# Holding each batch's loads to its tile, and reordering the first feed-forward tile, in an attention and ReGLU kernel

## The chip, the cores and the metric

The kernel runs on one core of a Trainium2 chip. The metric is the device time of one execution in microseconds; smaller is better. A core has five engines with queues of their own: TensorE (PE, with its weight loads shown as PEld), VectorE (DVE), ScalarE (ACT), GpSimd (POOL) and SyncE (SP). SP, ACT and POOL also issue DMAs. Each queue is worked off in order.

## The reference

Block-causal attention (a query sees the keys of its own block of 64 and of all earlier ones) over 8 batches, 8 heads, 576 positions and a head size of 64, followed by a gated feed-forward layer on all 4608 tokens. Inputs and output are float32.

```python
def _attn_ref(q, k, v):
    scores = scale * np.matmul(q, k.transpose(0, 1, 3, 2))
    mask = block_i >= block_j
    scores = np.where(mask, scores, -1000000000.0)
    scores = scores - np.max(scores, axis=-1, keepdims=True)
    attn = np.exp(scores)
    attn = attn / (np.sum(attn, axis=-1, keepdims=True) + 1e-09)
    return np.matmul(attn, v).astype(np.float32)

def _moe_ref(x, w_gate, w_val, w_out):
    gate = np.maximum(x @ w_gate, 0.0)
    val = x @ w_val
    return (gate * val @ w_out).astype(np.float32)
```

The attention output, transposed to (batch, position, head x size), is x: 4608 x 512. w_gate and w_val are 512 x 1536, w_out is 1536 x 512.

## The kernel before, in words

**Feed-forward tiles.** Everything is computed in bf16 with sums in float32. The 512 leading positions of each batch make one feed-forward tile (tiles 0 to 7); the last 64 positions of all eight batches make tile 8. `ffn_gen` (L566) is a generator that issues one tile after the other, and each `yield` follows one matmul. A tile has 144 such steps: steps 0 to 95 are the products with w_gate and w_val (twelve column groups f, for each four contraction chunks c of gate and four of val; L572), steps 96 to 143 are the products with w_out (four output groups s of twelve steps; L631). After a gate group comes a ReLU on ACT (L582), after a val group a product on DVE that writes hT (L588) and is put in the list `products`. A finished output group is copied to a buffer `ob` on DVE (L665) and stored by a DMA from ACT (L558). In tile 0 the first two output groups are different: their steps f = 0 to 7 go into two banks, are copied into `ob` as side sums (L651), and f = 8 to 11 go into banks of their own and are added to `ob` (L662). In tiles 0 and 1 the groups f = 0 and 1 are interleaved, two of them in score banks.

**Attention rounds.** A round r is one pair of heads of batch r // 4. `visit` (L368) issues its eight score products into two pairs of score banks ("sc") and into a third place (a bank "one" and a bank "ffnp"), and gives back three exponentials on ACT (L391, L397). `corners` (L446) zeroes the masked corners. `head_av` (L504) multiplies one head's weights with v on TensorE (L495) and normalises on DVE (L460, L461) into xnat; `both_av` (L518) does two heads in score banks. xnat is transposed into xT, the feed-forward input, either on TensorE (`to_xT_pe`, L533) or by a transposing DMA from SP (`to_xT_dma`, L544, issued at L547). Round r gives chunk c = r % 4 of the xT of its batch. The last 64 positions of a batch have a `tail_visit`, two `tail_av` and a transposing DMA into xTt (L489).

**PSUM.** Eight banks: two score tiles of two banks ("sc"), one bank "one", three banks "ffnp". The three ffnp banks serve the feed-forward groups, the third place of a visit, the head products with v, the transposes of `pe_mains` and to_xT for two of four rounds.

**Bringing in q, k and v.** Batches 0, 1 and 2 come by float32 loads from SP into ten stage buffers (class `Early`, L107), and are cast to bf16 on POOL, DVE or ACT. For batches 0 and 1 `pe_mains` (L232) transposes q and k of one pair of heads on TensorE and copies them to qTm and kTm (L244) on two engines; `pe_tails` does it for the last 64 positions. Batch 2 is transposed by SP's DMAs into "perm" and unpermuted by DVE and POOL. Batches 3 to 7 are loaded and cast in one step by POOL's DMAs (`load_qkv`, L266: five for q, five for k, five for v, issued at L278), then transposed by `dma_transposes` (L287) from SP. An argument `behind` makes the first DMA of the group wait for a given instruction. The bf16 buffers of q and k are doubled, those of v go by b % 2.

**Weights.** `load_w_half` loads the 512 columns i of w_gate and w_val in two halves of 256 columns, each half for all four contraction chunks, in runs of 1 KB. `load_w` loads w_out in runs of 2 KB. `cast_w` casts a stage buffer on a given engine (L327).

**The order.** The schedule is by hand. Each engine executes in the order in which the program issues. The start (L699 to L782) is written out in full; after it, `run` (L789) takes a list of events, each with a position p (a count of generator steps from a base), advances the generator to base + p and performs the event. A position of 0 to 143 with base 0 is a step of tile 0; tile j has base 144 j. `round_at(p, r, av, to_xT, after)` (L794) makes the events of a round: the visit and its first two exponentials at p, the third at p + after[0], the corners at p + after[1], the products with v at av, the transposition at to_xT. For batches 3 to 7 the loop at L897 places, in the tile before their own, the batch's rounds and, from position 120, its tail events, and also the loads of batch b + 1: q and k at position 9, v at position 46, `dma_transposes(b + 1)` at 66. Only for b = 3 (the loads of batch 4) is the first DMA held behind `products[-1]`, the last product on DVE that the program has issued by then. Positions order an engine against its own queue only; SP and POOL run ahead as far as data and buffers allow.

Of the kernel before, what the change touches and what calls it, by code (L numbers as in the profile page):

```python
# [17 lines left out]
def kernel(  # L18
# [88 lines left out]
    class Early:  # L107
# [124 lines left out]
        def pe_mains(self, hp, evac):  # L232
            for t in range(2):
                tp = psum_ffn.tile([128, 512], BF, name="ffnp")
                src = self.half(t, hp // 2)
                lo = 128 * (hp % 2)
                for j in range(4):
                    nc.tensor.transpose(  # L238
                        tp[:, 128 * j : 128 * j + 128], src[:, j, lo : lo + 128], ident
                    )  # L240
                for eng, c0, c1 in (
                    evac[t] if isinstance(evac[t], list) else [(evac[t], 0, 4)]
                ):
                    eng(  # L244
                        (qTm, kTm)[t][self.b % 2][:, c0:c1, hp, :].rearrange(
                            "p c (n j) -> p c n j", j=4
                        ),
                        tp.rearrange("p (j c n) -> p c n j", j=4, c=4)[:, c0:c1],
                    )
# [68 lines left out]
    def load_w_in(i):  # L318
        cols = slice(512 * i, 512 * i + 512)
        return load_w(wg[i], moe_w_gate[:, cols], 0) + load_w(wv[i], moe_w_val[:, cols], 0)  # L320
# [245 lines left out]
    def ffn_gen():  # L566
        for j in range(B + 1):
# [50 lines left out]
            for f in range(first, 12):  # L618
                gate = psum_ffn.tile([128, 512], FP, name="ffnp")
                val = psum_ffn.tile([128, 512], FP, name="ffnp")  # L620
                for t in range(2):
                    for c in range(4):
                        product((gate, val)[t], t, c, f)
                        if (t, c) == (0, 3):
                            gate_sb = relu(gate)
                        if (t, c) == (1, 3):
                            hidden(gate_sb, val)
                        yield

            def out_mm(op, s, f, n0, n1, lo, hi):  # L630
                nc.tensor.matmul(  # L631
                    op,
                    hT[f][:, 128 * s : 128 * (s + 1)],
                    wo[f // 4][:, f % 4, n0:n1],
                    start=(f == lo),
                    stop=(f == hi - 1),
                )

            def new_ob(n):
                return sb.tile([128, 512], FP, name="ob", bufs=4)[:, 0:n]  # L640

            part_sum = {}
            if j == 0:
                ops = [psum_ffn.tile([128, 512], FP, name="ffnp") for _ in range(2)]
                for f0 in (0, 4):
                    for s in range(2):
                        for f in range(f0, f0 + 4):
                            out_mm(ops[s], s, f, 0, 512, 0, 8)
                            if f == 7:
                                part_sum[s] = new_ob(512)  # L650
                                nc.vector.tensor_copy(part_sum[s], ops[s])  # L651
                            yield
            for s, n0, n1 in outs(j):
                op = psum_ffn.tile([128, 512], FP, name="ffnp")[:, 0 : n1 - n0]
                lo = 8 if s in part_sum else 0
                for f in range(lo, 12):
                    out_mm(op, s, f, n0, n1, lo, 12)
                    if f < 11:
                        yield
                if s in part_sum:  # L660
                    ob = part_sum[s]
                    nc.vector.tensor_tensor(out=ob, in0=ob, in1=op, op=AX.add)  # L662
                else:
                    ob = new_ob(n1 - n0)
                    nc.vector.tensor_copy(ob, op)  # L665
                if store:
                    store.pop()()
                store.append(lambda j=j, s=s, ob=ob, n=(n0, n1): put(j, s, ob, *n))
                yield
# [27 lines left out]
    with tc.manual_schedule(engines={E.PE, E.DVE, E.Activation, E.Pool, E.SP}):  # L697
# [54 lines left out]
        w_2 = [load_w_half(2, g) for g in range(2)]  # L752
# [15 lines left out]
        for g in range(2):  # L768
            cast_w(w_2[g], pool)
# [7 lines left out]
        for h0 in (4, 6):  # L777
            e1.cast_qk(h0, 2, (pool, None))
# [78 lines left out]
        def load_tails():  # L857
            e2.load_tails((0, 1))
            e2.load_tails((2,))

        events = round_at(96, 4, (120, 120.1), (125, pe_xT), (6, 11))
        events += round_at(104, 5, (127, 127.1), (131, pe_xT), (6, 15))
        events += round_at(126, 6, (138.2, 139), (146, pe_xT), (4, 9))
        events += round_at(138, 7, (148, None), (153, pe_xT), (3, 8))
        events += [
            (80, lambda: e1.cast_qk(0, 4, (None, dve))),
            (93, lambda: e1.pe_mains(0, (dve, act))),
            (95, lambda: e1.pe_mains(1, (dve, act))),
            (112.05, lambda: cast_w(last_w[1:], dve)),
            (119, lambda: e1.cast_qk(4, 2, (None, act))),  # L870
            (120.2, lambda: e1.cast_qk(6, 2, (None, act))),
            (123, lambda: e1.pe_mains(2, (dve, act))),
            (129, lambda: e1.pe_mains(3, (dve, act))),
# [23 lines left out]
        for b in range(3, B):  # L897
# [6 lines left out]
            if b + 1 < B:  # L904
                for at, which in ((9, (0, 1)), (46, (2,))):
# [4 lines left out]
                                b + 1, w, products[-1] if b == 3 and w == (0, 1) else None  # L910
# [35 lines left out]
```

## Time and profile before

| what | value |
|---|---|
| median of 8 runs | 370.11 us (368.33 to 372.95) |
| the profiled execution | 369.96 us |
| its span in the profile | 368.2 us |
| PE busy | 356.5 us (97%) |
| DVE, ACT, POOL busy | 170.5, 169.7, 112.4 us |
| mean granted clock of TensorE | 0.994 |
| HBM read, written | 37.75 MB, 9.44 MB |

Times in the profile count from the start of the span. In a timeline a line has a start, a length, an engine (a "q" after it is the engine's own queue, SPq and POOLq for issued DMAs), a line of the kernel, the operation, the tile written and the tiles read, how many were merged into it, and in brackets the idle time of the engine before it with what ended it. Matmuls overlap in their pipelines: the length of one, 0.38 us for 512 columns, is longer than the distance between two starts, so stalls are read from starts.

### The profile page before, as it was taken

To read this page: it belongs to the slowest core of one execution; us is meant where nothing else is said; L and a number is where in the kernel's file an instruction comes from. 1 tells how busy PE (TensorE), PEld (TensorE's weight loads), DVE (VectorE), ACT (ScalarE), POOL (GpSimd) and SP (SyncE) were. 2 spreads that over 40 slices of the span, in tenths; PEclk is the share of its full clock that TensorE was granted. 3 is DMA by queue.
4 is the path that set the end of the run, shared out by engine and by line. 5 is a ranking of instruction groups with operands and counts; after the bars stand their busy time and mean duration, and the time that the engine had idled before them with its cause. 6 is when DMAs were issued, how large, how long until landed. Compare 5 with 4: busy or idle time off the path is not lost.

```text
span 368.2 us, 7461 instructions
## 1 busy us (share of the span) xinstructions
PE 356.5 (97%) x2963; PEld 176.8 (48%) x2963; DVE 170.5 (46%) x395; ACT 169.7 (46%) x279; POOL 112.4 (31%) x145
## 2 busy tenths in 40 slices
PE   6999989999999999899999999999999999999995
PEld 2544445554554445344544455445544454444443
DVE  4744465475534544444345434554345434433422
ACT  4833746577245733466245643554455333302310
POOL 6666655389229912820085004000000000000000
PEclk9899999999999999999999999999999999999999
DMA  8999999999999999998299749565400420020013
GB/s 253 288 349 357 320 247 293 226 110 117 128 227 138 136 146 167 159 117 162 85 111 133 138 120 83 33 87 140 71 17 14 73 80 0 0 87 28 0 42 103
DMA packets 151363, 49.58 MB, mean 135 GB/s; under 512 B 132768, under 2 KB 145312, under 8 KB 151328
## 3 DMA queue, kind: packets, MB, share of 16 engines
q0 software_dynamic: 70320, 8.85, 55.0%
q1 hardware_dynamic: 75728, 31.08, 40.4%
q10 hardware_dynamic: 5280, 9.18, 8.2%
q8 instruction: 23, 0.38, 0.5%
q14 instruction: 12, 0.10, 0.1%
HBM read 37.75 MB, written 9.44 MB: 128 GB/s over the span
## 4 chain that ended last, share of the span: by engine, by line
PE 91%; DMA 3%; DVE 3%; ACT 1%; issue 0%; ACTq 0%
PE ffnp L572 51%; PE ffnp L631 24%; PE ffnp L495 5%; PE sc L382 3%; DMA xT<-xnat 2%; PE ffnp L475 2%; PE one L382 1%; PE ffnp L238 1%; PE sc L416 1%; DMA stage<-in_q_dram 1%; PE sc L339 1%; DVE xnat L461 1%; PE sc L572 0%; PE one L416 0%; DVE ob L662 0%
## 5 line engine op out<-in xcount | busy, mean ns | idle before, releaser
L588 DVE TENSOR_TENSOR hT<-gate_sb,ffnp 128x512 bf16<-128x512 bf16 x106 | 72.7, 686 | 97.2 <-PE ffnp L572 80.7
L582 ACT ACTIVATE gate_sb<-ffnp 128x512 bf16<-128x512 f32 x108 | 64.6, 600 | 104.0 <-PE ffnp L572 103.9
L572 PE MATMUL ffnp<-xT,wg 128*128 128x512 bf16 x384 | 103.7, 379 | 1.8 <-DMA xT<-xnat 1.7
L631 PE MATMUL ffnp<-wo,hT 128*128 128x512 bf16 (+1 forms) x444 | 101.5, 373 | 1.3 <-DVE wo L327 0.9
L572 PE MATMUL ffnp<-xT,wv 128*128 128x512 bf16 x376 | 101.1, 379 | 0.0
L572 PEld LDWEIGHTS <-wg 128*128 128x128 bf16 x432 | 40.2, 98 | 47.0 <-issue 4.5
L572 PEld LDWEIGHTS <-wv 128*128 128x128 bf16 x432 | 39.9, 98 | 46.6 <-issue 3.8
L631 PEld LDWEIGHTS <-hT 128*128 128x128 bf16 x444 | 40.9, 98 | 43.2 <-issue 2.3
L391 ACT ACTIVATE attnT<-sc 128x1024 bf16<-128x1024 f32 x56 | 56.9, 1036 | 0.0
L665 DVE COPY ob<-ffnp 128x512 f32<-128x512 f32 (+1 forms) x35 | 23.7, 676 | 39.4 <-PE ffnp L631 39.3
L278 POOL DMA_DIRECT2D v_bf<-in_v_dram x25 | 21.1, 874 | 63.6 <-PE ffnp L475 63.6
L495 PEld LDWEIGHTS <-attnT 128*128 128x128 bf16 x640 | 26.0, 98 | 14.3 <-DVE xnat L461 3.8
L460 DVE RECIPROCAL recip<-ffnp 128x4 f32<-128x4 f32 (+1 forms) x73 | 13.1, 179 | 34.9 <-PE ffnp L495 23.1
L495 PE MATMUL ffnp<-v_bf,attnT 128*128 128x65 bf16 x570 | 26.4, 194 | 0.0
L461 DVE TENSOR_TENSOR xnat<-ffnp,recip 128x256 bf16<-128x256 f32 x57 | 24.2, 424 | 2.2 <-DVE recip L460 0.3
L397 ACT ACTIVATE attnT<-one 128x256 bf16<-128x256 f32 x28 | 10.7, 383 | 30.5 <-PE ffnp L382 27.8
L278 POOL DMA_DIRECT2D q_bf<-in_q_dram x20 | 17.9, 936 | 14.1 <-issue 14.1
L437 ACT ACTIVATE attnTt<-one 64x256 bf16<-64x256 f32 x8 | 3.0, 377 | 36.0 <-PE ffnp L416 36.0
L278 POOL DMA_DIRECT2D k_bf<-in_k_dram x20 | 17.9, 928 | 1.6 <-DMA v_bf<-in_v_dram 1.5
L382 PE MATMUL sc<-qTm,kTm 64*128 64x512 bf16 (+1 forms) x168 | 17.2, 305 | 0.0
L382 PEld LDWEIGHTS <-kTm 64*128 64x128 bf16 x224 | 9.5, 94 | 15.4 <-issue 11.5
L428 ACT ACTIVATE attnTt<-sc 128x1024 bf16<-128x1024 f32 x16 | 15.7, 1014 | 0.0
(87 smaller groups left out, 245.4 us busy)
## 6 DMA issues: line engine op xcount, KB each, us to landing
out_dram<-ob ACTq DMA_DIRECT2D x32, 256.0 KB, 2.6
stage<-in_moe_w_gate_dram SPq DMA_DIRECT2D x6, 512.0 KB, 9.2
stage<-in_moe_w_val_dram SPq DMA_DIRECT2D x6, 512.0 KB, 8.8
stage<-in_moe_w_out_dram SPq DMA_DIRECT2D x6, 512.0 KB, 9.5
q_bf<-in_q_dram POOLq DMA_DIRECT2D x20, 128.0 KB, 6.8
k_bf<-in_k_dram POOLq DMA_DIRECT2D x20, 128.0 KB, 6.9
v_bf<-in_v_dram POOLq DMA_DIRECT2D x20, 128.0 KB, 6.0
stage<-in_v_dram SPq DMA_DIRECT2D x19, 128.0 KB, 5.0
```

Of the source, the lines that this page charges most:

```text
L278: ins = nc.gpsimd.dma_start(dst, src[b, :, 128 * c : 128 * c + n, :].rearrange("h p d -> p h d"),)
L382: nc.tensor.matmul(where[c].rearrange("p (c n) -> p c n", n=128), kTm[b % 2][head_of(hh), c, hp, :], qTm[b % 2][head_of(hh), c:4, hp, :], ...
L391: return lambda: nc.scalar.activation(at[:, :, lo : lo + 512], sc, AF.Exp, scale=scale)
L428: return lambda: nc.scalar.activation(at[:, :, 2 * i : 2 * i + 2, 0:256], main[i].rearrange("p g (h n) -> p g h n", h=2), AF.Exp, scale=scale,
L460: nc.vector.reciprocal(recip, av[:, :, 64])
L461: nc.vector.tensor_tensor(out=out, in0=av[:, :, 0:64], in1=recip.to_broadcast([rows, n, 64]), op=AX.mult,)
L495: nc.tensor.matmul(av[:, p, :], at[:, col : col + 128], v_bf[b % 2][:, c, h, :], start=(p == 0), stop=(c == p), skip_group_check=True,)
L572: nc.tensor.matmul(to, (wg, wv)[t][f // 4][:, c, 128 * (f % 4) : 128 * (f % 4) + 128], x[:, c], start=(c == 0), stop=(c == 3),)
L582: nc.scalar.activation(gate_sb, gate, AF.Relu)
L588: nc.vector.tensor_tensor(out=h, in0=gate_sb, in1=val, op=AX.mult)
L631: nc.tensor.matmul(op, hT[f][:, 128 * s : 128 * (s + 1)], wo[f // 4][:, f % 4, n0:n1], start=(f == lo), stop=(f == hi - 1),)
L665: nc.vector.tensor_copy(ob, op)
```

## The change

It touches six places.

- `pe_mains` takes an optional pair of banks `two`. Without it, it takes both ffnp banks at once before the first transpose; all eight transposes are issued ahead of the copies. The new `mains_1` gives it the two banks of a score tile, for batch 1's first three pairs of heads.
- Part 2 of w_gate and w_val is loaded by rows (`load_w_rows`: 256 rows of all 512 columns, runs of 2 KB) in place of columns. Of the four casts the last is split: one half on POOL, the other on ACT at position 67. In tile 0 the group f = 8 takes its steps in the order gate c = 0, 1, val c = 0, 1, gate c = 2, 3, val c = 2, 3.
- In tile 0 the first two output groups keep their two banks over all twelve steps each, in turns of four; no side sum is copied, and no group is added. All outputs end in `finish`, a copy and the store.
- Round 5's visit moves from position 104 to 112, its third exponential and its corners with it; its products with v move to 128, its transposition to 132. Batch 1's `pe_mains` move from 93, 95, 123, 129 to 91, 92.5, 122.5, 130.
- The casts of k for heads 4 to 7 of batch 1 move from ACT (positions 119 and 120.2) to POOL's written-out part.
- The loads of batches 5, 6 and 7 are held behind `products[-1]` as those of batch 4 were.

```diff
-        def pe_mains(self, hp, evac):
+        def pe_mains(self, hp, evac, two=None):
+            if two is None:
+                two = [psum_ffn.tile([128, 512], BF, name="ffnp") for _ in range(2)]
             for t in range(2):
-                tp = psum_ffn.tile([128, 512], BF, name="ffnp")
                 src = self.half(t, hp // 2)
                 lo = 128 * (hp % 2)
                 for j in range(4):
                     nc.tensor.transpose(
-                        tp[:, 128 * j : 128 * j + 128], src[:, j, lo : lo + 128], ident
+                        two[t][:, 128 * j : 128 * j + 128],
+                        src[:, j, lo : lo + 128],
+                        ident,
                     )
+            for t in range(2):
                 for eng, c0, c1 in (
...
+    def load_w_rows(i, g):
+        sts = []
+        for dst, src in ((wg, moe_w_gate), (wv, moe_w_val)):
+            st = new_stage(1024).rearrange("p (c n) -> p c n", c=2)
+            nc.sync.dma_start(
+                st,
+                src[256 * g : 256 * g + 256, 512 * i : 512 * i + 512].rearrange(
+                    "(c p) f -> p c f", p=128
+                ),
+            )
+            sts.append((dst[i][:, 2 * g : 2 * g + 2], st))
+        return sts
...
+                steps = [(t, c) for t in range(2) for c in range(4)]
+                if (j, f) == (0, 8):
+                    steps.sort(key=lambda e: e[1] // 2)
...
-            part_sum = {}
-            if j == 0:
-                ops = [psum_ffn.tile([128, 512], FP, name="ffnp") for _ in range(2)]
-                for f0 in (0, 4):
-                    for s in range(2):
-                        for f in range(f0, f0 + 4):
-                            out_mm(ops[s], s, f, 0, 512, 0, 8)
-                            if f == 7:
-                                part_sum[s] = new_ob(512)
-                                nc.vector.tensor_copy(part_sum[s], ops[s])
-                            yield
...
+            groups = outs(j)
+            while groups:
+                some = 2 if j == 0 and len(groups) == 4 else 1
+                ops = [
+                    psum_ffn.tile([128, 512], FP, name="ffnp")[:, 0 : n1 - n0]
+                    for _, n0, n1 in groups[:some]
+                ]
+                for f0 in (0, 4, 8) if some == 2 else (0,):
+                    for op, (s, n0, n1) in zip(ops, groups):
+                        for f in range(f0, f0 + 4 if some == 2 else 12):
+                            out_mm(op, s, f, n0, n1)
+                            if f == 11:
+                                finish(op, s, n0, n1)
+                            yield
+                groups = groups[some:]
...
-        w_2 = [load_w_half(2, g) for g in range(2)]
+        w_2 = [load_w_rows(2, g) for g in range(2)]
...
-        for g in range(2):
-            cast_w(w_2[g], pool)
+        cast_w(w_2[0] + w_2[1][:1], pool)
+        halves = [[a[:, c : c + 1] for a in w_2[1][1]] for c in range(2)]
+        cast_w(halves[:1], pool)
...
-            e1.cast_qk(h0, 2, (pool, None))
+            e1.cast_qk(h0, 2, (pool, pool))
...
+        def mains_1(hp, evac=(dve, act)):
+            two = psum_sc.tile([128, 2, 1024], BF, name="sc")
+            e1.pe_mains(hp, evac, [two[:, t, 0:512] for t in range(2)])
+
-        events += round_at(104, 5, (127, 127.1), (131, pe_xT), (6, 15))
+        events += round_at(112, 5, (128, 128.1), (132, pe_xT), (4, 14))
...
+            (67, lambda: cast_w(halves[1:], act)),
             (80, lambda: e1.cast_qk(0, 4, (None, dve))),
-            (93, lambda: e1.pe_mains(0, (dve, act))),
-            (95, lambda: e1.pe_mains(1, (dve, act))),
+            (91, lambda: mains_1(0)),
+            (92.5, lambda: mains_1(1)),
             (112.05, lambda: cast_w(last_w[1:], dve)),
-            (119, lambda: e1.cast_qk(4, 2, (None, act))),
-            (120.2, lambda: e1.cast_qk(6, 2, (None, act))),
-            (123, lambda: e1.pe_mains(2, (dve, act))),
-            (129, lambda: e1.pe_mains(3, (dve, act))),
+            (122.5, lambda: mains_1(2)),
+            (130, lambda: e1.pe_mains(3, (dve, act))),
...
-                                b + 1, w, products[-1] if b == 3 and w == (0, 1) else None
+                                b + 1, w, products[-1] if w == (0, 1) else None
```

## The prediction, made before the result was known

> **What bounds the kernel now.** I read the table of stages first: one row for each tile of the feed-forward part, after 39 us of start. Columns: stretch, its length, busy time of each engine with the instruction count, TensorE clock, DMA share, GB/s.
>
> ```profile
> 39.01:61.19 22.18, 20.31 (x200) 10.77 (x199) 12.38 (x31) 15.43 (x27) 12.91 (x16) 1.00 1.02 267
> 61.19:104.10 42.91, 42.74 (x446) 21.87 (x445) 23.50 (x59) 22.27 (x38) 24.20 (x27) 1.00 1.82 173
> 104.10:145.36 41.26, 41.15 (x418) 21.24 (x417) 19.28 (x48) 21.71 (x36) 21.50 (x26) 1.00 2.04 150
> 145.36:186.06 40.70, 39.01 (x338) 19.09 (x336) 17.96 (x44) 19.38 (x32) 12.59 (x16) 1.00 1.54 134
> 186.06:224.69 38.63, 38.63 (x337) 19.02 (x336) 17.96 (x44) 19.17 (x32) 12.58 (x16) 1.00 1.29 120
> 224.69:263.31 38.62, 38.62 (x337) 19.02 (x336) 17.96 (x44) 19.17 (x32) 3.67 (x5) 1.00 0.77 90
> ```
>
> The last three rows hold the same TensorE work (336 weight loads). The two undisturbed ones take 38.63 and 38.62 us, the row of tile 3 takes 40.70. So TensorE sets the pace, 38.63 us is the floor of such a tile, and tile 3 loses 2.07 us. From 186 us to the end there is nothing left to win but in the last stores, which the change leaves alone. What can move lies before 186 us.
>
> Next the order of time on TensorE at the head of tile 3, and SP's and POOL's queues before it:
>
> ```profile
> 146.20 0.60 PE L382 MATMUL sc<-qTm,kTm 64*128 64x512 bf16 x6
> 147.33 0.38 PE L572 MATMUL ffnp<-xT,wg 128*128 128x512 bf16 x1 [0.53 <-DMA xT<-xnat]
> 148.83 0.38 PE L572 MATMUL ffnp<-xT,wg 128*128 128x512 bf16 x1 [1.13 <-DMA xT<-xnat]
> ```
>
> ```profile
> 128.71 6.31 SPq L290 DMA_TRANSPOSE kTm<-k_bf  x1
> 135.12 1.37 SPq L294 DMA_TRANSPOSE kTt<-k_bt  x1
> 136.58 4.47 SPq L547 DMA_TRANSPOSE xT<-xnat  x3
> ```
>
> ```profile
> 120.91 3.62 POOL L278 DMA_DIRECT2D q_bf<-in_q_dram  x4
> 126.47 2.71 POOL L278 DMA_DIRECT2D k_bf<-in_k_dram  x3 [0.36 <-DMA v_bf<-in_v_dram]
> 133.37 0.69 POOL L278 DMA_DIRECT2D k_bt<-in_k_dram  x1 [4.19 <-DMA q_bf<-in_q_dram]
> ```
>
> The chunks c = 2 and c = 3 of xT are late: the chain of waits shows the last transposing DMA from 139.84 for 8.95 us, where the median is 3.8. POOL's ten loads between 120.9 and 134 are batch 5's q and k, issued two tiles ahead because nothing holds them once batch 4's are out.
>
> Last the order of time on TensorE in the second half of tile 0:
>
> ```profile
> 39.64 0.38 PE L238 MATMUL ffnp<-ident,k_bf 128*128 128x128 bf16 x4 [0.25 <-ACT gate_sb L582]
> 44.58 2.55 PE L631 MATMUL ffnp<-wo,hT 128*128 128x512 bf16 x11
> 47.98 1.24 PE L631 MATMUL ffnp<-wo,hT 128*128 128x512 bf16 x5 [0.86 <-DVE wo L327]
> 50.24 0.81 PE L631 MATMUL ffnp<-wo,hT 128*128 128x512 bf16 x3 [0.41 <-DVE ob L662]
> 51.44 0.38 PE L238 MATMUL ffnp<-ident,k_bf 128*128 128x128 bf16 x4 [0.16 <-DVE xnat L461]
> ```
>
> Unit prices from undisturbed places: a 512-column step 0.2158 us (77 steps from 22.39 to 39.01), eight transposes 0.44, a visit's eight score products 0.75, one head's products with v 0.30, one to_xT 0.22. From position 93 (39.01) to the end of tile 0 (61.19): 51 steps 11.01, four pe_mains 1.76, four visits 3.00, six heads 1.80, two to_xT 0.44, tail transposes 0.60; sum 18.61, measured 22.18: 3.57 us of stalls. By gaps between starts: first two pe_mains 0.41 and 0.19, first visit 0.20, the last wo cast 1.03, the side sum of ob 0.57, third pe_mains 0.33, fourth 0.51, the rest 0.33.
>
> **What the Trainium skill says.** "Perfetto Trace Analysis", section Identifying the Most-Contended Engine: matmul busy share is a poor measure of distance from the limit. The trace agrees: tile 1's row is 42.74 of 42.91 busy, though the unit prices (31.08 + 10.4 for four visits, two tail visits, 14 groups of products with v, two to_xT) give about 41.5. So I count from starts. "DMA: Bandwidth & Descriptors", section Issuing engines are not separate DMA queues: DMAs of SP and POOL run on the same 16 engines. The trace agrees, by the 8.95 us above. Same page, Why small descriptors are slow: about 3 cycles on top of 32-byte beats; my estimate for 2 KB runs in place of 1 KB is 67/70, 4%. Here loads in 1 KB runs (w_gate, w_val) feed POOL's casts every 1.50 us, those in 2 KB runs (w_out) every 1.36: 9%, so I use the measured one, as the favourable end.
>
> **The change, part by part.**
>
> *Held loads.* Batch 4's were held already, at 108.45. For 5, 6 and 7 the first q load waits for the DVE product last emitted at position 9 of their tile. Behind it in POOL's queue stand only 14 more loads; every corner memset of those tiles is on DVE. Tile 2 loses ten of its 25 loads. Tile 3 issues 15 (now: 5 of v and 10 of q and k between 144.8 and 158.7, again 15), tile 4 15 as now, tile 5 15 where it now has 5. No tile then has more than tile 4 has today, and tile 5 starts after that at its floor. Batch 4's last load is out at 121.03; xT of round 15 is issued at 139.9 on a quiet DMA, lands in 2.4 to 3.8, before 144, and is read at 146.5 (145.36 + two steps + a visit). Gain 2.07; bounds 0 and 2.07. Are the late loads in time? In tile 3 q and k go out from 2.3 to about 11.5 us into the tile and land about 7 later, by 18.5. SP issues batch 5's transposing DMAs only after xT of round 17, which sits 19.5 us into the tile (164.93). They take 7 to 8 us as in tiles 3 to 5, then rounds 18 and 19 (ready at 24 and 33) follow. Cost taken: 0; the rival below has the other end.
>
> *Weight loads by rows.* Same bytes, same four loads. The half of w_2 that was needed at position 80 (36.2 us) is now needed at 68 to 71. The casts now end at 29.84, 31.35, 32.86; the fourth begins at 33.29. Needed: val c = 0 at 33.18, gate c = 2 at 33.6, val c = 2 at 34.04, c = 3 at 34.26 (position 64 is at 32.75). The split fourth cast: 0.62 on POOL ends at 33.91, 0.62 on ACT the same, before f = 8's relu (34.2). Margin 0.13 us if the data come no sooner; with 1.36 in place of 1.50 for four loads they and all behind them come 0.56 sooner. Taken: no cost and no gain; bounds +0.4 and -0.5.
>
> *pe_mains in score banks.* Same 24 transposes. No ffnp bank is waited for, so 0.60 of stalls go. ACT's queue then holds kTm copy (0.59), f = 11's relu (0.60), kTm copy (0.59): the second copy ends at 41.0. The visit would reach its second score bank at 40.95, so 0.1 stays, where 0.20 was.
>
> *No side sums, visit 5 later.* Removed: two DVE copies of 0.69; the adds (0.69) become copies (0.69). The matmul count is the same. The copies stood ahead of the last wo cast (47.12 to 47.93). Without them it runs when its data land, about 44.5, and ends by 45.4; it is needed at 46.2 (visit 4 at 40.5, 16 steps, visit 5, three steps). 1.03 goes. Next late: at position 120 (47.27) batch 1's v cast, which ends at 47.65 on POOL behind DMA, and the bank of the second group, whose copy ends at 48.25. I take 0.43, where 0.57 was. If another bank is handed out it is 0.3 to 0.7.
>
> *k casts to POOL.* Two of 0.62 go between POOL's waits for DMA (1.18 and 2.29 us), so nothing shifts, and ACT no longer waits 1.18 and 1.85 in its queue for them. The third pe_mains at 48.7 meets a k cast ending at 49.1: 0.15, where 0.33 was. The fourth still needs two ffnp banks behind normalise: 0.5, unchanged.
>
> *Tails.* At 57.9 the tail transposes meet batch 1's k tail, cast at 58.24: new, 0.3. The rest of tile 0 keeps 0.2.
>
> Stalls left: 0.1 + 0.43 + 0.15 + 0.5 + 0.3 + 0.2 = 1.7. Gain of tile 0: 3.57 - 1.7 = 1.87. Tile 1 begins 1.9 us sooner, and its unpermuting copies then meet the transposing DMAs of batch 2 (landed by 77.2): DVE may wait 1 us at 75 but has 1.38 idle behind it, and visit 10, which needs them, comes at 86.8. Tiles 1 and 2 move whole.
>
> Sum: 369.96 - 2.07 - 1.87 = 366.0 for the profiled execution (span 368.2 and 1.8 around it). That execution lies 0.15 under the median of 370.11, so 366.1.
>
> **Rivals.** *DMA arrivals take back tile 0* (0.17). From 4 to 52 us the DMA runs at 240 to 390 GB/s and POOL waits for it before most casts. If v, k and tails come no sooner than TensorE needed them before, only the held loads pay: 369.96 - 2.07 = 367.9. Against it: v needed at 47.3, there at 47.65, and so on through the list. *The xT wait stays* (0.07): SP's own queue or batch 4's loads make it late: 369.96 - 1.87 = 368.1. Against it: the last POOL load lands long after batch 4's. *Everything pays* (0.12): arrivals 0.56 sooner leave 0.6 of stalls: 369.96 - 2.07 - 2.97 = 364.9. *Slower* (0.06): held loads are late for SP's transposing DMAs, SP's queue is in order, and the last two xT of each of tiles 3 to 5 stand behind. In tile 2 it took from 108.45 to 136.5, 28 us, from first load to last of these DMAs. Begun 2.5 us into a tile that is 30.5, plus 2.4 to issue two xT, plus the worst landing seen, 9.3: 42.2, against 39.8 when c = 2 is read. 2.4 us three times, less the gains: 369.96 + 7.2 - 3.9 = 373.3. It decides from 28.1 us into the tile on; the 28 us were with 25 loads in flight, tiles 3 and 4 with 15 took 7 to 8 for these DMAs. That the hold does nothing is excluded: POOL sat idle 14.06 us before batch 4's first load.
>
> **Numbers.** Forecast 0.58 (366.1, own spread 365.3 to 367.2). Within 0.5% (1.9 us) is about what measurement cannot tell from no change. Faster by more takes the forecast, the all-pays case and most of the first two rivals: 0.84; same 0.10; slower 0.06. Range 364.8 to 368.2.
>
> **What would show it.** No DMA wait at tile 3's head, and that tile at 38.6; POOL's loads of batches 5 to 7 some 2.5 us into tiles 3, 4, 5; no gap before the last wo product; tile 1 beginning near 59.3; tiles 4 and 5 still 38.63. Wrong if a tile after 3 exceeds 39, if steps at positions 64 to 72 wait for wv, or if position 142 waits over 1 us for a tail cast.

## The result and the profile after

The changed kernel takes 366.95 us (median of 11 runs, 366.05 to 368.75). The kernel before, run on the same chips, takes 370.18 us (32 runs, 368.33 to 373.07). The ratio is 0.9911, with a 95% interval of 0.9885 to 0.9936: 2.4 to 4.3 us less. Ratios leave out executions that took over 1.5% longer than the fastest of the same kernel; of all the kernels below that concerns two of late_60's four. The profiled execution of the changed kernel takes 367.69 us and its span is 365.7 us, against 369.96 and 368.2 before.

The same table of stages as in the prediction, now of the changed kernel, with stretches cut at the starts of its own tiles. The first row begins at the first `pe_mains`, two steps of 0.2158 us earlier in the order than the first row of before did. Columns: stretch, its length, busy time of PE, PEld, DVE, ACT and POOL with the instruction count, TensorE clock, DMA share, GB/s.

```profile
39.56:60.99 21.43, 20.25 (x202) 10.71 (x201) 10.98 (x30) 14.04 (x25) 13.06 (x18) 1.00 0.97 254
60.99:103.90 42.91, 42.74 (x445) 21.86 (x444) 23.59 (x59) 22.27 (x38) 24.78 (x28) 1.00 1.60 177
103.90:144.93 41.03, 41.03 (x417) 21.22 (x416) 19.29 (x48) 21.51 (x36) 12.58 (x15) 1.00 1.45 138
144.93:183.57 38.64, 38.64 (x338) 19.00 (x337) 17.96 (x44) 19.17 (x32) 12.58 (x15) 1.00 1.34 120
183.57:222.21 38.64, 38.64 (x338) 19.02 (x337) 17.97 (x44) 19.17 (x32) 12.58 (x15) 1.00 1.41 120
222.21:260.84 38.63, 38.63 (x337) 19.04 (x336) 17.96 (x44) 19.17 (x32) 12.58 (x15) 1.00 1.50 121
```

Tile 3, the fourth row, has fallen from 40.70 to 38.64 us, the length of its neighbours. POOL's column shows what moved: tile 2 has 15 instructions where it had 26, and from there on every tile has 15. The second half of tile 0, the first row, has lost a little over one microsecond, when the two extra steps (0.43) are taken off: 22.18 before, 21.00 now. Tile 1 is unchanged and tile 2 is 0.23 shorter.

The head of tile 3 on TensorE, in the changed kernel. Columns: start, length, engine, line, operation, tile written and tiles read, how many were merged.

```profile
144.93 0.59 PE L585 MATMUL ffnp<-xT,wg 128*128 128x512 bf16 x2
...
146.11 0.60 PE L585 MATMUL ffnp<-xT,wg 128*128 128x512 bf16 x2
```

Neither chunk of xT is waited for, where 0.53 and 1.13 us stood in brackets before. SP's queue ahead of it:

```profile
131.64 8.96 SPq L560 DMA_TRANSPOSE xT<-xnat  x3
```

And POOL's queue after it, in the same columns:

```profile
148.86 3.51 POOL L282 DMA_DIRECT2D q_bf<-in_q_dram  x4 [27.98 <-DVE hT L601]
```

Batch 5's first load now goes out at 148.86 instead of 120.91. POOL stood idle for 27.98 us before it, and what ended that was DVE's product into hT: the hold. SP's last three transposing DMAs of xT are issued from 131.64 to 140.60, the last of them at nearly the same time as before (139.42, where it was 139.84). What changed is the time from issue to landing. In the kernel before, for these three:

```profile
DMA to landing us min/median/max: 9.0/9.2/9.3
```

In the changed kernel, for the two of the three whose landing its trace holds:

```profile
DMA to landing us min/median/max: 2.4/2.4/2.4
```

The last one lands at 141.82 in place of 148.79, well before TensorE comes to it.

The second half of tile 0 on TensorE in the changed kernel:

```profile
42.55 0.39 PE L395 MATMUL sc<-qTm,kTm 64*128 64x384 bf16 x4 [0.42 <-ACT kTm L248]
42.88 3.63 PE L646 MATMUL ffnp<-wo,hT 128*128 128x512 bf16 x16
...
47.09 1.90 PE L646 MATMUL ffnp<-wo,hT 128*128 128x512 bf16 x8
...
49.77 0.59 PE L646 MATMUL ffnp<-wo,hT 128*128 128x512 bf16 x2 [0.17 <-DVE ob L656]
...
52.21 0.28 PE L395 MATMUL one<-qTm,kTm 64*128 64x256 bf16 x1 [0.32 <-ACT kTm L248]
```

The same stretch on ACT:

```profile
40.94 0.59 ACT L248 COPY kTm<-sc 128x512 bf16<-128x512 bf16 x1 [2.09 <-DVE qTm L248]
41.42 0.60 ACT L595 ACTIVATE gate_sb<-ffnp 128x512 bf16<-128x512 f32 x1
41.91 0.59 ACT L248 COPY kTm<-sc 128x512 bf16<-128x512 bf16 x1
...
51.57 0.59 ACT L248 COPY kTm<-sc 128x512 bf16<-128x512 bf16 x1 [2.33 <-DVE qTm L248]
```

And on DVE:

```profile
40.21 1.35 DVE L248 COPY qTm<-sc 128x512 bf16<-128x512 bf16 x2 [0.34 <-PE sc L239]
...
45.39 0.43 DVE L340 CAST wo<-stage 128x512 bf16<-128x512 f32 x1
```

The wait of 0.86 us for the last wo cast is gone: DVE casts at 45.39, and TensorE passes from visit 5 (46.44) to its next eight steps at 47.09 without a bracket. Two waits are new, 0.42 and 0.32 us, both for ACT's copy of k, and the bracket in ACT's lines tells what ACT itself had waited for: not TensorE's transposes, but DVE's copy of q. DVE's first copy of q runs from 40.21 to about 40.9, and ACT's copy of k begins at 40.94. This is the part that the prediction did not have.

### The profile page after: what moved, and what is told of

It reads as the page before. It is cut to its first block, busy times and chain, and to the rows that moved or that the text cites. A ratio compares the mean times of both kernels' runs of the same rounds, so it can differ in the third digit from the quotient of the medians.

```text
span 365.7 us, 7455 instructions
## 1 busy us (share of the span) xinstructions
PE 357.2 (98%) x2963; PEld 177.0 (48%) x2963; DVE 169.2 (46%) x393; ACT 168.5 (46%) x278; POOL 113.5 (31%) x147
## 4 chain that ended last, share of the span: by engine, by line
PE 94%; ACT 2%; DVE 2%; DMA 1%; issue 0%; ACTq 0%
PE ffnp L585 51%; PE ffnp L646 26%; PE ffnp L508 5%; PE sc L395 3%; PE ffnp L488 3%; PE one L395 2%; PE sc L429 1%; PE sc L352 1%; DMA stage<-in_q_dram 1%; ACT attnT L368 1%; PE ffnp L239 1%; DVE qTm L248 1%; PE sc L585 0%; PE one L429 0%; PE one L508 0%
## 5 line engine op out<-in xcount | busy, mean ns | idle before, releaser
L646 PEld LDWEIGHTS <-hT 128*128 128x128 bf16 x444 | 40.9, 98 | 42.0 <-issue 1.1
L656 DVE COPY ob<-ffnp 128x512 f32<-128x512 f32 (+1 forms) x37 | 25.1, 677 | 41.5 <-PE ffnp L646 41.5
```

The source lines that it names most:

```text
L646: nc.tensor.matmul(op, hT[f][:, 128 * s : 128 * (s + 1)], wo[f // 4][:, f % 4, n0:n1], start=(f == 0), stop=(f == 11),)
```

## The experiments

All kernels are compared with the kernel before, run on the same chip. The table gives the median, the ratio with its 95% interval, and, from one profiled execution each, the lengths of tiles 0 and 3 between the first w_gate products of successive tiles. The ratios are as recorded and are not quotients of the two medians, from which they differ by up to 0.0016 (late_60: by 0.0095). A tile's length is not the same in every execution: hold_only has the tile 0 of the kernel before, unchanged, and shows 43.47. Three groups share a chip each: no_hold, hold_only, apart and apart_4 the first (before: 370.27 there), wo_early, no_rows, k_on_act and late_60 the second (369.83), hold_wo, late_30 and best the third (369.56).

| kernel | median us (runs) | ratio to before | tile 0 | tile 3 |
|---|---|---|---|---|
| before | 370.18 (32) | | 43.87 | 40.70 |
| after | 366.95 (11) | 0.9911 [0.9885, 0.9936] | 42.67 | 38.64 |
| no_hold | 369.24 (22) | 0.9968 [0.9952, 0.9984] | 42.68 | 39.83 |
| hold_only | 368.06 (8) | 0.9928 [0.9902, 0.9954] | 43.47 | 38.63 |
| apart | 366.06 (6) | 0.9870 [0.9838, 0.9902] | 42.34 | 38.63 |
| apart_4 | 365.71 (6) | 0.9862 [0.9832, 0.9892] | 41.60 | 38.64 |
| wo_early | 369.65 (22) | 0.9995 [0.9975, 1.0015] | 42.84 | 41.16 |
| no_rows | 367.04 (7) | 0.9913 [0.9881, 0.9945] | 42.74 | 38.63 |
| k_on_act | 366.83 (7) | 0.9913 [0.9875, 0.9951] | 42.61 | 38.64 |
| late_60 | 394.19 (4) | 1.0564 [1.0475, 1.0652] | 42.91 | 45.66 |
| hold_wo | 366.81 (6) | 0.9935 [0.9910, 0.9960] | 42.85 | 38.64 |
| late_30 | 366.96 (6) | 0.9928 [0.9902, 0.9954] | 42.71 | 38.63 |
| best | 365.70 (6) | 0.9899 [0.9876, 0.9921] | 41.16 | 38.64 |

**The theory** after the result: the held loads pay their 2.07 us in full; of tile 0's gain most comes from the one cast that is no longer queued behind the side sums; and the score banks lose what they should have won, because the copies of q and k out of one score tile run one after the other. **The rivals**: the score banks wait for the transposes or for ACT's relu, not for DVE; the data of batch 1 and the rows of w_gate and w_val set the pace; the casts of k on POOL are what helps or hurts.

### The hold: taken away, and alone

no_hold is the changed kernel with the hold as it was:

```diff
-                                b + 1, w, products[-1] if w == (0, 1) else None
+                                b + 1, w, products[-1] if b == 3 and w == (0, 1) else None
```

> The changed kernel, with only the hold on the loads of batches 5, 6 and 7 taken back. Theory (the hold pays by itself, at the head of tile 3): batch 5's q and k go out in tile 2 again, the last two xT are late, tile 3 is 40.7 us long instead of 38.64, tiles 4 and 5 stay at 38.6, and the time is 2.1 us over the changed kernel's: 369.1. Rival (the wait went because tile 0's changes moved the DMAs): tile 3 stays at 38.6 and the time at 367.0.

hold_only is the kernel before with the opposite edit of that line and nothing else.

> The kernel before, with only the hold added. Theory: tile 3 falls from 40.70 to 38.6 us, tile 0 is as before, the time 368.1 (2.1 under 370.2). Rival: the DMA wait at the head of tile 3 stays, 370.2.

Measured: 369.24 us without the hold. That is 2.3 above the changed kernel (measured in another set of runs), with intervals of the ratios that do not meet (0.9952 to 0.9984 against 0.9885 to 0.9936). With the hold alone 368.06, ratio 0.9902 to 0.9954, which is 1.7 to 3.6 us less than before. In no_hold the xT wait comes back on TensorE, at the third step of tile 3, which begins at 145.86:

```profile
146.51 0.60 PE L395 MATMUL sc<-qTm,kTm 64*128 64x512 bf16 x6
148.24 0.59 PE L585 MATMUL ffnp<-xT,wg 128*128 128x512 bf16 x2 [1.14 <-DMA xT<-xnat]
```

It is 1.1 us in this execution instead of 1.66. In hold_only nothing of the kind is left and tile 3 takes 38.63. So the mechanism of this part stands, and a size of somewhat over 2 us in the medians. A single profile gives the size less well: without the hold tile 3 takes 39.83 (no_hold), 40.70 (before) and 41.16 (wo_early), that is 1.2 to 2.5 us more than with it.

### The loads held longer: how much room there is

Two kernels move the held loads to later positions of their tile. late_30 moves q and k from 9 to 30, late_60 moves q and k to 60 and v to 62:

```diff
-                for at, which in ((9, (0, 1)), (46, (2,))):
+                for at, which in ((30, (0, 1)), (46, (2,))):
```

```diff
-                for at, which in ((9, (0, 1)), (46, (2,))):
+                for at, which in ((60, (0, 1)), (62, (2,))):
```

> The changed kernel, with q and k of the next batch held to position 30 in place of 9, v at 46. It asks where the slower case begins. Theory (k lands about 25 us into the tile, the transposing DMAs of q and k end about 32, the last xT lands at 38.3, and 39.8 is needed): just in time, tiles 3 to 5 at 38.6 to 39, 367.0 to 368. Rival (the transposing DMAs take 7 to 8 us each while v's loads are in flight, as with the loads at 60): 1 to 4 us at each of four tile heads, 372 to 382.

> The changed kernel, with the held loads later: q and k of the next batch at position 60 of a tile in place of 9, v at 62 in place of 46. This tries the rival of a slower kernel: k lands about 32 us into the tile, SP issues the last of the transposing DMAs of q and k at about 36, and the last two xT stand behind it in SP's queue and land at 42, where 39.8 is needed: 2.2 us in each of the next four tile heads, 375.8 (372 to 380). Against it (there is room even so): 367.0.

late_30 measured 366.96, the same as the changed kernel. SP's queue in it, with tile 3 begun at 143.79:

```profile
166.69 7.15 SPq L294 DMA_TRANSPOSE kTm<-k_bf  x1
173.93 1.20 SPq L298 DMA_TRANSPOSE kTt<-k_bt  x1
175.22 2.55 SPq L560 DMA_TRANSPOSE xT<-xnat  x2
```

The last transposing DMA of q and k ends 31.3 us into the tile, and the two of xT behind it are still in time for tile 4 at 182.42.

late_60 measured 394.19, far above the 375.8 expected. TensorE's waits in it (us in total, times, longest):

```profile
PE one L395 <- DMA kTm<-k_bf: 12.4, 3, 6.1
PE ffnp L585 <- DMA xT<-xnat: 6.1, 4, 2.9
```

And its SP queue near the end of tile 3, which lasts from 143.68 to 189.34:

```profile
180.54 7.90 SPq L294 DMA_TRANSPOSE kTm<-k_bf  x1
...
189.82 4.09 SPq L560 DMA_TRANSPOSE xT<-xnat  x2
```

Its four times spread from 388.40 to 394.74 and the profiled one is among the longest, so the lines serve for the kind of wait, not for its exact size. The kind is the rival's: the held loads are late for SP's transposing DMAs, and xT stands behind them in SP's queue. The expectation had counted xT alone. Here k itself is late for the next tile's first visit, and that is the larger wait. TensorE then loses more than the wait: after the one of 6.11 us the six score products take 1.06 us instead of 0.60, and the granted clock of tiles 3 and 4 is 0.93. The Trainium skill, "TensorE: Matmul & The Clock Gate", Part 1: The HAM clock gate, says that the array falls back to half of its clock when it has been idle for a window of about 3.4 us. The trace agrees for this gap, which was longer than that: the products behind it ran at about half speed. But it took less at the head of tile 3, where behind gaps of 2.94 and 1.14 us four w_val products took 1.91 us instead of 1.03. So the rival "slower" is a real mechanism; its place begins somewhere between the positions of late_30 and those of late_60, and this kernel's position 9 is clear of it.

### The last wo cast alone

wo_early is the kernel before with one cast of w_out on DVE ahead of the second side sum; hold_wo is the same with the hold of every batch.

```diff
-            (112.05, lambda: cast_w(last_w[1:], dve)),
+            (107.5, lambda: cast_w(last_w[1:], dve)),
```

> The kernel before, with the last cast of w_out on DVE issued at position 107.5 in place of 112.05, ahead of the two side-sum copies. Theory (that cast was late because it stood behind two copies of 0.69 us, not because its data were): it runs when the data land, about 44.5, the gap of 1.03 us ahead of position 115 goes, the gap at position 120 stays, tile 0 is 42.9 us long instead of 43.87, the time 369.2. Rival (the load bounds it): 370.2.

> The kernel before, with the hold on the loads and with the last w_out cast on DVE at position 107.5. It tells why the earlier cast alone moved the time so little (369.65 against 369.83) though its tile 0 was 1.03 us shorter: there tile 3 was longer by 0.46. Theory (the time saved in tile 0 was in part given back at the DMA wait of tile 3 and in part hidden by the scatter of the start): with the hold tile 3 is 38.6 whatever tile 0 does, so tile 0 is 42.8 and the time 1.0 under the kernel with the hold alone: 367.1. Rival (loads that arrive at a fixed time take the gain back in tiles 0 and 1): tile 0 is shorter but the median stays at 368.0.

Tile 0 takes 42.84 us in wo_early and 42.85 in hold_wo, 1.03 less than in the profile of before and within 0.2 of the changed kernel's 42.67. On TensorE in wo_early the 0.86 has gone and the wait for the side sum stays:

```profile
45.25 3.63 PE L631 MATMUL ffnp<-wo,hT 128*128 128x512 bf16 x16
...
49.90 0.81 PE L631 MATMUL ffnp<-wo,hT 128*128 128x512 bf16 x3 [0.41 <-DVE ob L662]
```

How much the late cast cost differs between executions. In hold_only the cast stands behind the two side sums as before, but TensorE waits for it 0.47 us and not 0.86, and tile 0 is 0.4 us shorter than in before. There the cast itself takes 0.42 us (48.99 to 49.41). In the profile of before it takes 0.81 (47.12 to 47.93), beside a cast of q on POOL (from 47.59) that also takes 0.81, where the same cast takes 0.61 in hold_only. In no_hold, again beside casts on POOL, it takes 1.16, there without making TensorE wait. Why casts on the two engines are slow together was not followed up. Apart from this wait, TensorE's starts in tile 0 agree in before and hold_only within 0.1 us. So 0.39 of the 1.03 belongs to that one execution. From hold_only to hold_wo, which begin tile 0 at 19.20 and 19.24, the earlier cast alone takes 0.62 us from tile 0, and from hold_only to no_hold (19.24), which has all of the change but the hold, it is 0.79.

The median of wo_early does not show it: 369.65 against 369.83 on that chip, interval 0.9975 to 1.0015, where 369.2 was expected. In its profile tile 3 takes 41.16 instead of 40.70, so the wait for xT took back about half; whether that is the rule without the hold, one profile cannot tell, and no_hold, whose cast is early too, had a tile 3 of 39.83 and kept a ratio below 1. With the hold, hold_wo comes to 366.81. On the same chip late_30, which is the whole change with later loads, comes to 366.96. The two intervals lie on each other: as far as these runs can tell, two edits of a line each give what the whole change gives. But the interval of hold_only (0.9902 to 0.9954) lies there too. The medians do not show the cast's part of this; the wait that is gone and the length of tile 0 do.

### The score banks: q and k in different tiles

apart is the changed kernel with the bank of k for batch 1's first three head pairs taken from another PSUM tile than that of q; apart_4 does the fourth pair too, in the "one" bank and an ffnp bank.

```diff
-            two = psum_sc.tile([128, 2, 1024], BF, name="sc")
-            e1.pe_mains(hp, evac, [two[:, t, 0:512] for t in range(2)])
+            q_bank = psum_sc.tile([128, 2, 1024], BF, name="sc")[:, 0, 0:512]
+            if hp == 0:
+                k_bank = psum_one.tile([128, 1024], BF, name="one")[:, 0:512]
+            elif hp == 1:
+                k_bank = psum_ffn.tile([128, 512], BF, name="ffnp")
+            else:
+                k_bank = psum_sc.tile([128, 2, 1024], BF, name="sc")[:, 0, 0:512]
+            e1.pe_mains(hp, evac, [q_bank, k_bank])
```

The further edit of apart_4 is cut to its main lines:

```diff
+            if hp == 3:
+                q_bank = psum_one.tile([128, 1024], BF, name="one")[:, 0:512]
...
+            elif hp in (1, 3):
...
-            (130, lambda: e1.pe_mains(3, (dve, act))),
+            (130, lambda: mains_1(3)),
```

> The changed kernel, with q and k of batch 1's first three pairs of heads transposed into two different PSUM tiles (q in a score tile; k in the bank one, in an ffnp bank and in a second score tile) instead of the two banks of one score tile. In the changed kernel ACT's copy of k starts only as DVE's copy of q ends (40.94 after 40.21 + 0.69, 51.57 after 50.84 + 0.69), though they read different banks. Theory (copies out of one tile are put in order, and this costs the visits of rounds 4 and 6 their waits of about 0.5 and 0.38 us): ACT copies at once, both waits fall under 0.1, tile 0 ends 0.8 us sooner, 366.2. Rival (ACT is late because of its own queue): the copies stay where they are, 367.0.

> As the kernel with different PSUM tiles for q and k, and the fourth pair of heads (position 130) goes into the bank one and one ffnp bank instead of two ffnp banks. Theory: its wait for banks that the normalisation of round 5 frees (0.59 us in the changed kernel) goes too, 365.7, the fastest of all. Rival (another step is late then, k's cast or the tails): the gain of the first three pairs only, 366.2.

ACT's copies of k in apart_4:

```profile
39.16 0.59 ACT L248 COPY kTm<-one 128x512 bf16<-128x512 bf16 x1 [1.36 <-PE one L239]
...
40.14 0.59 ACT L248 COPY kTm<-ffnp 128x512 bf16<-128x512 bf16 x1
...
49.70 0.59 ACT L248 COPY kTm<-sc 128x512 bf16<-128x512 bf16 x1 [2.09 <-PE sc L239]
```

They wait for TensorE now and not for DVE. DVE's two copies of q run from 38.94 to 40.29 in this execution, so the first copy of k lies beside them. Both new waits of TensorE are gone, and the fourth pair's too: among TensorE's waits from tile 0 on, the only one that the profile still lists at 0.2 us or more is 0.2 for a cast of k. apart measured 366.06 and apart_4 365.71, 0.9 and 1.2 us below the changed kernel's median, which comes from another set of runs.

The single profile of apart shows less of it, since its feed-forward part begins at 16.72 instead of 18.32 (the last section has this) and meets data that are not there yet. At positions 64 to 72 one pair of w_gate steps starts at 33.16 and the w_val steps after it at 33.89, 0.73 instead of 0.43 (POOL's cast of its part of the last w_val rows ends at 33.83); and tile 1 takes 43.27 instead of 42.91. Two profiles with the same start are better compared: no_hold (19.24) has q and k in one score tile, best below (19.23) has them apart (and the weights by columns, which changes nothing, as the next experiment shows). Their tiles 0 take 42.68 and 41.16, 1.5 us less, and their tiles 1 the same 42.91. Read from starts as in the table of the next section, the first two pe_mains with visit 4 lose 0.01 us in best where the changed kernel loses 0.60, visit 6 loses nothing in place of 0.38, and the fourth pe_mains 0.04 in place of 0.59. That is 1.52 together.

### The rows and the casts of k

no_rows is the changed kernel with part 2 of w_gate and w_val loaded by columns again and f = 8 in the old order; k_on_act casts batch 1's k for heads 4 to 7 on ACT at positions 119 and 120.2 again.

```diff
-                if (j, f) == (0, 8):
-                    steps.sort(key=lambda e: e[1] // 2)
...
-        w_2 = [load_w_rows(2, g) for g in range(2)]
+        w_2 = [load_w_half(2, g) for g in range(2)]
...
-        cast_w(w_2[0] + w_2[1][:1], pool)
-        halves = [[a[:, c : c + 1] for a in w_2[1][1]] for c in range(2)]
-        cast_w(halves[:1], pool)
+        for g in range(2):
+            cast_w(w_2[g], pool)
```

```diff
-            e1.cast_qk(h0, 2, (pool, pool))
+            e1.cast_qk(h0, 2, (pool, None))
...
+            (119, lambda: e1.cast_qk(4, 2, (None, act))),
+            (120.2, lambda: e1.cast_qk(6, 2, (None, act))),
```

> The changed kernel, with part 2 of w_gate and w_val loaded and cast in column halves again and the steps of f = 8 in the old order. Theory (loading by rows brings later data forward by about half a microsecond, on which TensorE waits little, and puts a deadline at position 70 that is missed by up to 0.3 us when the start is quick): no clear difference, 366.6 to 367.4; POOL's casts after it 0.3 to 0.6 later; no wait at position 70. Rival (data behind it bound tile 0): tile 0 0.5 us longer, 367.5.

> The changed kernel, with the casts of k for heads 4 to 7 of batch 1 on ACT again, at positions 119 and 120.2. Theory (in the changed kernel ACT stands idle 2.33 us before the third copy of k, waiting for DVE's copy of q, so both casts fit there): 0 to 0.2 longer, 367.0 to 367.2. Rival (ACT's wait for the load of k holds up the copies and the exponentials behind it): 0.5 us longer, 367.5.

Both medians, 367.04 and 366.83, lie within 0.12 us of the changed kernel's, and tile 0 takes 42.74 and 42.61 against 42.67. Neither part carries anything that these runs can measure. The intervals reach 1.2 and 1.4 us to either side, so a smaller difference would not be seen in the times; the lengths of tile 0 are the closer comparison. The rows do come sooner: POOL's casts of them start 1.36 us apart (28.79, 30.14 and 31.50), where in the kernel before it is 1.5 (28.80, 30.31 and 31.82). Batch 1's v cast then starts at 46.12, where it was 46.60 before and is 46.46 in no_rows. But TensorE was not waiting for those data.

### Put together

best has the score banks of apart_4 and loads by columns as in no_rows.

> The kernel with q and k of all four pairs of heads in different PSUM tiles, and with part 2 of w_gate and w_val in column halves as in the kernel before. Theory (rows bring nothing, and their deadline at position 70 costs up to 0.3 us when the start is quick): 365.5, the same as with rows (365.7) or up to 0.3 less. Rival (with tile 0 shorter, the data that rows bring forward by half a microsecond count): 366.2.

365.70 us, the same as apart_4 (365.71), and 1.26 below late_30 on the same chip. Tile 0 is the shortest of all, 41.16. The intervals of these two ratios (0.9832 to 0.9892 and 0.9876 to 0.9921) overlap that of the changed kernel, so that they are faster than it rests on the medians and on the traces together.

## Why the prediction was right, and which term was mis-sized

The forecast of 366.1 us stands beside 366.95: the direction, the range and the two places were right, and the gain was 3.2 us instead of 4.0. The forecast's own ratio, 366.1 / 370.11 = 0.989, lies in the measured interval, so the medians alone would not show a miss. The traces do.

**Held loads: -2.07.** Right, in mechanism and size: tile 3 lost 2.06, hold_only gave 2.2 in medians on its chip and no_hold took 2.3. The landing fell from 8.95 us to 2.4, as written. That 2.07 came out to a hundredth is luck, since the wait of another profile would have given 1.2 or 2.5. Two details differed without effect. POOL's loads begin 3.9 us into tile 3 instead of 2.3, and batch 5's transposing DMAs take 9.9 us (162.44 to 172.34) instead of 7 to 8. They end 27.4 us into the tile. The rival put its point of decision at 28.1, so the room looked thin; late_30 ends at 31.3 and loses nothing: the two xT, out by 177.77, then had some 6 us until they were read (183.6 to 183.8), and needed no more, where the rival had assumed 9.3. The point lies later than it was put.

**The last wo cast: -1.03.** Right in the mechanism: earlier in DVE's queue, the cast makes TensorE wait no more. The size holds for the one profile from which it was read; 0.39 of it was a slow cast there, and between executions with like starts the earlier cast is worth 0.62. It is most of what tile 0 won: wo_early alone brings tile 0 to 42.84.

**pe_mains in score banks: the term that failed.** The prediction wrote: "No ffnp bank is waited for, so 0.60 of stalls go", and of the visit: "so 0.1 stays". It had ACT's queue right, but took ACT's first copy to begin when the transposes were done, as it did before, when q and k lay in two ffnp tiles. Both now lie in one score tile of two banks. In the built program ACT's copy waits for DVE's in place of TensorE, and the profile shows the wait by name. The Trainium skill, "PSUM — Partial Sum Buffer", section PSUM bank collisions raise a hardware error, says that two engines on different banks run clean. The trace of apart_4 agrees, where a copy of q and one of k run at the same time out of two banks: the order came from sharing a tile, not from the chip. ACT's first copy thus began some 0.7 us late, and relu and second copy with it.

The stalls of the stretch from 39.56 to 60.99, read from starts as in the prediction (21.43 less 19.04 of unit prices, which are the 18.61 of the prediction and two steps):

| place | predicted | measured |
|---|---|---|
| first two pe_mains and visit 4 | 0.1 | 0.60 |
| the second group's bank | 0.43 | 0.35 |
| third pe_mains | 0.15 | 0 |
| visit 6, behind the third pe_mains | 0 | 0.38 |
| fourth pe_mains | 0.5 | 0.59 |
| tails | 0.3 | 0 |
| rest | 0.2 | 0.45 |
| sum | 1.7 | 2.4 |

Visits 4 and 6 alone are 0.88 too much. The tails and the third pe_mains were put 0.45 too high, since k's casts came in time; the small places together were put 0.26 too low. Tile 0 won 1.20 instead of 1.87, both against the profile of before with its slow cast; against hold_only's 43.47 it is 0.8.

**Weight loads by rows, and k casts to POOL: 0.** Right; no_rows and k_on_act differ from the changed kernel by no more than runs do.

**Tiles 1 and 2 move whole.** Right for tile 1 (42.91 both times). Tile 2 became 0.23 shorter, at one visit about 14 us into it. It did so in every kernel in which the last wo cast was early (41.02 to 41.04) and not with the hold alone (41.25). Why was not followed up.

**Tile 1 beginning near 59.3.** It begins at 60.99 in this profile. Of the 1.7 us, 0.67 are the stalls above, and 1.00 is a later start of the whole feed-forward part, 18.32 instead of 17.32, in code that the change leaves alone.

**The rivals.** *DMA arrivals take back tile 0*: excluded for the changed kernel: tile 0's remaining waits are for work of DVE and ACT, and no_rows does not matter. *The xT wait stays*: excluded by the head of tile 3. *Everything pays*, 364.9: not reached; apart_4 and best come closest at 365.7, with the banks apart. *Slower*: real, but beyond position 30, and then much dearer than 2.4 us per tile: tiles 3 to 5 of late_60 take 45.66 to 46.16, 7 us more. Of the three signs of being wrong none came in the changed kernel, where the steps at positions 64 to 72 start 0.43 apart in pairs; in apart, with its quicker start, one of these pairs was 0.30 late.

## What to carry to other kernels

When two engines drain what one group of matmuls wrote, look at what their copies wait for, not only at the banks: here two banks of one PSUM tile were copied one after the other, and two tiles side by side, and TensorE lost 0.98 us at the two places behind it. Before a rebuild of a stage, move by itself the one instruction that stands in the wrong place of its queue: a cast and a hold, a line each, gave all of the gain that these runs can tell from the whole change. And loads that run far ahead are not free: held until their tile, they left the DMA to the transfer that TensorE was about to wait for; but the hold has an end: with the loads at position 60 four tiles paid 6 to 7.5 us each, where the old wait cost about 2.

## What was not expected of the hardware

The start is not the same from one execution to the next. The first w_gate product comes between 16.72 and 19.24 us in the profiles of these kernels, although the code ahead of it is nearly the same in all. An early visit on TensorE in the kernel before:

```profile
6.26 0.86 PE L339 MATMUL sc<-qTm,kTm 64*128 64x512 bf16 x6 [0.56 <-DVE qTm L244]
```

And the same visit in the changed kernel:

```profile
6.32 1.20 PE L352 MATMUL sc<-qTm,kTm 64*128 64x512 bf16 x6 [0.36 <-DVE qTm L248]
```

The same six products take 0.86 in one and 1.20 in the other: they ran at half speed for a longer time there. The Trainium skill, "TensorE: Matmul & The Clock Gate", Part 1: The HAM clock gate, says that the warm-up depends on the phase of a free-running window and is "run-variable". The traces agree, though the stretches seen here are longer than its 3.4 us: in best four transposes still take 0.61 us at 16.80, and 0.40 at 18.69. The later start hid 1.0 us of a gain of 3.5 when the two profiles were compared end to end, and it is a reason to compare tile by tile. A quick start is not all gain either: the three kernels whose tile 1 began before 59.5 us, apart, apart_4 and no_rows, needed 43.27, 43.09 and 43.23 us for it, and the others 42.91 to 42.95. Data that arrive at a fixed time would do this; what TensorE waited for there was not followed up.
